# First MLP: one activation function in place of a chain of three, and seven block products in place of eight

## The chip, the cores and the metric

One core of a Trainium2 chip runs the whole program. The metric is the device time of that core in microseconds (us), lower is better; before the change the median of 3 runs is 575.84 us (575.25 to 576.12). TensorE (PE) multiplies, VectorE (DVE), ScalarE (ACT) and GpSimd (POOL) work element by element, SyncE (SP) issues the transfers. Products land in PSUM, everything else lies in SBUF.

## The reference

A decaying linear attention over 2 x 768 tokens gives x (1536 x 512), and two MLPs follow:

```
h = x @ w_in                       # 512 -> 2048
sp = where(h > 20, h, log1p(exp(min(h, 20))))
x = (h * tanh(sp)) @ w_out         # 2048 -> 512
h = x @ w_in2
r = maximum(h, 0)
out = (r * r) @ w_out2
```

The function h * tanh(softplus(h)) of the first MLP is known as Mish. All arrays are fp32, and the result has to be as exact as fp32 allows.

## The kernel before

Each fp32 operand is split into a high part (rounded, type fp32r) and a low part (what is left): ACT copies the high part, DVE subtracts (`split`, L248). A product of two such operands is three matmuls: high by low, low by high, high by high (`mm3`). All matmuls of the MLPs are 128 x 128 (stationary) by 128 x 512 (moving).

The 1536 tokens are three blocks t = 0, 1, 2 of 512. The hidden 2048 channels are four groups g of 512. For each MLP (L = 0, 1) and each group the kernel loads and splits two weight tiles for the way up (kind 0) and two for the way down (kind 1), forms h (`up`), applies the activation and splits the result (`take`, `gated`), multiplies down (`down`) and adds to an accumulator (`ac`). `up` of one block is 48 matmuls, and so is `down` of one block.

The second MLP already takes blocks 1 and 2 together (`up_pair`): with the block matrices of the weights and of x it forms seven products P1, P2, P6, P7, P5, P4, P3 (a Strassen-Winograd scheme) of 12 matmuls each, 84 in place of 96. For that DVE forms four differences T1 to T4 of the x blocks once per MLP (`forms`; seven operands are then split into fh and fl), four sums S of the weights once per group (`sums`; tiles s, then sh and sl), and seven additions per group that put the products together (tiles u and h). `STRASSEN` (L33) says which MLP does so.

The first MLP's activation before is a chain: DVE takes min(h, 20) into z (L568), ACT applies Sigmoid, Arctan and Sin to z (L571), DVE multiplies h by z, then the split gives gh and gl. Sigmoid and Arctan share one table set of ACT, Sin has another, so ACT loads tables (ACT_TABLE_LOAD).

The order of the work is set by a planner (`Plan`) when the program is built: each operation has an assumed duration, TensorE's have a rank, the others a due time derived from it; the planner gives each engine a fixed list, and 50 SBUF units of 128 x 1024 and four PSUM pairs of banks to the tiles. On the chip every engine works its list strictly in order and waits on semaphores. `LATE` says how many of a group's three `down` come after the next group's `up` of block 0.

Names: attention works on 12 chunks of 128 tokens; sc are its scores, a the masked scores, sd the state update, xo its output in PSUM, kv and qk the inputs; xh, xl are the split x, xr the x kept whole (block pair), st, m and t are weights as loaded and being decoded (L490, L493, L498), wh and wl the split weights, dn the product down, yh and yl the split input of the second MLP.

Of the kernel before, what the change touches and what calls it, by code (L numbers as in the profile page):

```python
# [12 lines left out]
F32 = mybir.dt.float32  # L13
# [4 lines left out]
ALU = mybir.AluOpType  # L18
# [11 lines left out]
RANGE = 2.0 ** -112  # L30

UNITS = 50
STRASSEN = (False, True)  # L33
DEBUG = None
SPARE = (10, 6)
AHEAD = 40.0
LATE = (1, 1, 0, 0)


class Val:  # L40
# [5 lines left out]


class Op:
    def __init__(self, eng, us, fn, name, rank, table, lag, due, spare):
        self.eng, self.us, self.fn, self.name, self.rank, self.table = eng, us, fn, name, rank, table  # L50
        self.lag, self.due, self.spare = lag, due, spare
        self.before, self.after, self.vals = {}, {}, {}
        self.late, self.start, self.end = math.inf, None, None


class Plan:
# [11 lines left out]
        self.ops, self.ahead = [], ahead  # L68
        self.wrote, self.used, self.orders = {}, defaultdict(list), set()

    def op(self, eng, us, fn, reads=(), writes=(), name="", rank=None, table=None, lag=None, due=None, spare=0):
        o = Op(eng, us, fn, name, rank, table, self.LAG[eng] if lag is None else lag, due, spare)
        for x in reads:
            o.before[self.wrote[x]] = None
        for x in writes:
            o.before.update(dict.fromkeys(self.used[x]))
            if x in self.wrote:
                o.before[self.wrote[x]] = None
        for x in reads:
            self.used[x].append(o)  # L80
        for x in writes:
            self.wrote[x], self.used[x] = o, []
        for x in (*reads, *writes):
            if isinstance(x[0], Val):
                o.vals[x[0]] = None
        for v in o.vals:
            v.left += 1
        for b in o.before:
            b.after[o] = None
        self.ops.append(o)  # L90
        return o
# [29 lines left out]
    def run(self, start, units):  # L121
        self.dues(start)
        free = {"S": list(range(units)), "P": list(range(4))}
        clock = dict.fromkeys(self.LAG, 0.0)
        left = {o: len(o.before) for o in self.ops}
        ready = {e: [] for e in self.LAG}
        for o in self.ops:
            if not left[o]:
                o.at = 0.0
                ready[o.eng].append(o)  # L130
        releases, table, order = [], [None], []
        now, n = 0.0, 0
        while n < len(self.ops):
            while releases and releases[0][0] <= now:
                _, v = releases.pop(0)
                free[v.space].append(v.slot)
            for e in ready:
                if clock[e] > now:
                    continue
                can = [o for o in ready[e] if o.at <= now and (e == "PE" or o.late - now < self.ahead[e])]  # L140
                if not can:
                    continue
                best = None
                for o in sorted(can, key=lambda o: o.rank if e == "PE" else
                                o.late + (2.6 if o.table and table[0] not in (None, o.table) else 0.0)):
                    need = defaultdict(int)
                    for v in o.vals:
                        if v.slot is None:
                            need[v.space] += 1
                    if all(len(free[s]) >= k + (o.spare if s == "S" else 0) for s, k in need.items()):  # L150
                        best = o
                        break
                if best is None:
                    continue
                o = best

                if e != "PE" and any(q.at > now and q.at < now + 0.7 * o.us and q.late < o.late - 2.0
                                     for q in ready[e]):
                    continue
                us = o.us  # L160
                if o.table:
                    us += 1.3 if table[0] != o.table else 0.0
                    table[0] = o.table
                for v in sorted((v for v in o.vals if v.slot is None), key=lambda v: v.name):
                    v.slot = free[v.space].pop(0)
                o.start, o.end = now, now + us
                clock[e] = o.end
                ready[e].remove(o)
                order.append(o)
                n += 1  # L170
                for v in o.vals:
                    v.left -= 1
                    v.was = max(v.was or 0.0, o.end + o.lag)
                    if not v.left:
                        bisect.insort(releases, (v.was, v), key=lambda r: r[0])
                for a in o.after:
                    left[a] -= 1
                    if not left[a]:
                        a.at = max(b.end + (b.lag if (b.eng != a.eng or b.lag > 1) and (b, a) not in self.orders else 0.0)
                                   for b in a.before)  # L180
                        ready[a.eng].append(a)
            times = [c for c in clock.values() if c > now]
            times += [o.at for r in ready.values() for o in r if o.at > now]
            times += [r[0] for r in releases[:1]]
            times += [o.late - self.ahead[e] + 1e-6 for e in ready if e != "PE" for o in ready[e]
                      if o.late - self.ahead[e] + 1e-6 > now]
            times = [t for t in times if t > now]
            if not times:
                stuck = [o.name for r in ready.values() for o in r][:20]
                held = sorted({v.name for o in self.ops for v in o.vals if v.slot is not None and v.left and v.space == "S"})  # L190
                raise RuntimeError(f"stuck {held} at {now} with {n} of {len(self.ops)}: {stuck} {len(free['S'])} {len(free['P'])}")
            now = min(times)
        self.order = order
        return order
# [3 lines left out]
def attention_mlps(ctx, tc, lam, qk, kv, w_in, w_out, w2_in, w2_out, out):  # L198
# [15 lines left out]
    NG = DFF // (GF * P)  # L214
    assert DM == NP * P and DM == TB and NK == GF == 4 and SEQ % 2 == 0 and NB == 3

    const = ctx.enter_context(tc.tile_pool(name="const", bufs=1))
    units = ctx.enter_context(tc.tile_pool(name="units", bufs=1))
    banks = ctx.enter_context(tc.tile_pool(name="banks", bufs=1, space=PSUM))
    dram = ctx.enter_context(tc.tile_pool(name="dram", bufs=1, space=bass.MemoryType.DRAM))  # L220
# [50 lines left out]


    W = 2 * CH
    neg_ln2 = const.tile([P, 1], F32, name="neg_ln2")
    tab_d = dram.tile([H, W], F32, name="tab_d")
    misc = Val("misc")
    mask = Val("mask")
# [34 lines left out]
    def ones():  # L312
        nc.vector.memset(tab()[:, 0 : CH - 1], 0.0)
        nc.vector.memset(tab()[:, CH - 1 : CH], 1.0)
        nc.vector.memset(neg_ln2, -math.log(2.0))

    op("ACT", 0.1, lambda: nc.scalar.dma_start(out=tab()[:, CH : CH + 1], in_=lam), [], [(misc, "lam")],
       name="lam", lag=2.2, due=0.0)
    op("DVE", 0.4, ones, [], [(misc, "tab"), ("neg_ln2", 0)], name="ones")
    op("DVE", 1.2, powers, [(misc, "lam")], [(misc, "tab")], name="powers")  # L320
    op("ACT", 0.1, lambda: nc.scalar.dma_start(out=tab_d, in_=tab()), [(misc, "tab")], [("tab_d", 0)],
       name="tab_d", lag=2.2, due=0.0)
# [236 lines left out]
    def gated(L, g, t, u, h, in_psum):  # L559

        name = f"{L}{g}{t}{u}"
        hi, lo = Val(f"gh{name}", dtype=F32R), Val(f"gl{name}", dtype=F32R)
        g_hi[L, g, t, u], g_lo[L, g, t, u] = hi, lo
        if L == 0:


            z = Val(f"z{name}")
            op("DVE", 0.8, lambda: nc.vector.tensor_scalar(  # L568
                out=tl(z), in0=tl(h), scalar1=20.0, scalar2=None, op0=ALU.min), [(h, 0)], [(z, 0)], name=z.name)
            for f, table, kw in ((AF.Sigmoid, "s", {"bias": neg_ln2}), (AF.Arctan, "s", {}), (AF.Sin, "t", {"scale": 2.0})):  # L570
                op("ACT", 1.05, lambda f=f, kw=kw: nc.scalar.activation(out=tl(z), in_=tl(z), func=f, **kw),  # L571
                   [(z, 0), ("neg_ln2", 0)], [(z, 0)], name=f"{f}{name}", table=table)
            op("DVE", 1.25, lambda: tt(tl(h), tl(h), tl(z), ALU.mult), [(h, 0), (z, 0)], [(h, 0)], name=f"g{name}")
        else:
            if not in_psum:
                op("ACT", 1.05, lambda: nc.scalar.activation(out=tl(h), in_=tl(h), func=AF.Relu),
                   [(h, 0)], [(h, 0)], name=f"r{name}")
            op("ACT", 1.05, lambda: nc.scalar.activation(out=tl(h), in_=tl(h), func=AF.Square),
               [(h, 0)], [(h, 0)], name=f"sq{name}")
        split(hi, lo, h, [(h, 0)])  # L580

    def take(L, g, t, u, src):
        h = Val(f"h{L}{g}{t}{u}")
        op("ACT", 1.05, lambda: nc.scalar.activation(out=tl(h), in_=tl(src), func=AF.Relu if L else AF.Copy),  # L584
           halves(src), [(h, 0)], name=h.name)
        gated(L, g, t, u, h, True)

# [242 lines left out]
```

## Time and profile before

| | |
|---|---|
| median of 3 runs | 575.84 us (575.25 to 576.12) |
| profiled execution | 575.08 us, its span 573.0 us |
| PE busy | 558.7 us (98%), 2970 matmuls |
| DVE busy | 378.8 us (66%) |
| ACT busy | 369.2 us (64%), of it 56.5 us in 44 table loads |
| POOL busy | 33.1 us (6%) |

The span is what the profiler saw from the first to the last instruction; the remaining 2.08 us lie around it. The attention fills the first 71 us, together with the first block's `up`; then the first MLP runs to about 319 us and the second to the end. Busy shares are averages over these stages; ends of matmuls are modelled, since they are pipelined: a matmul shows 389 ns, but the next one starts after 227 ns.

### The profile page before, as it was taken

How to read it: one execution, taken by the hardware profiler on the slowest of the kernel's cores; microseconds unless marked ns; L12 is line 12 of the kernel's file. 1: busy time of each engine (PE TensorE's matmuls, PEld its weight loads, DVE VectorE, ACT ScalarE, POOL GpSimd, SP SyncE). 2: the span in 40 equal slices, each digit the busy share in tenths (PEclk: the TensorE clock that was granted, in tenths of full speed). 3: DMA queues.
4: the chain of work that ended last, by engine and by line, in shares of the span. 5: the costliest groups of instructions: out<-in, count | busy, mean ns of one | idle time of the engine just before them, and what ended most of it. 6: DMA issues, size and time to landing. Idle time of an engine off the chain costs nothing.

```text
span 573.0 us, 7150 instructions
## 1 busy us (share of the span) xinstructions
PE 558.7 (98%) x2970; PEld 462.2 (81%) x2970; DVE 378.8 (66%) x414; ACT 369.2 (64%) x390; POOL 33.1 (6%) x31
## 2 busy tenths in 40 slices
PE   5899999999999999999999999999999999999997
PEld 2778888888888888888888887888888888888885
DVE  5656896358557686476398989852858677497622
ACT  2436678999978987987989678554624556147600
POOL 1564500000000000000000000000000000000000
PEclk9999999999999999999999999999999999999999
DMA  7998040401204031040303002021140123200022
GB/s 233 398 409 338 3 129 19 139 9 45 103 1 148 2 110 38 0 148 0 120 28 122 25 1 73 1 74 38 60 160 1 37 74 114 107 1 1 1 110 110
DMA packets 15999, 50.53 MB, mean 88 GB/s; under 512 B 1624, under 2 KB 3168, under 8 KB 15968
## 3 DMA queue, kind: packets, MB, share of 16 engines
q1 hardware_dynamic: 15936, 50.08, 25.0%
q8 instruction: 23, 0.38, 0.3%
q14 instruction: 8, 0.07, 0.0%
q10 hardware_dynamic: 32, 0.01, 0.0%
HBM read 46.92 MB, written 3.15 MB: 87 GB/s over the span
## 4 chain that ended last, share of the span: by engine, by line
PE 94%; DMA 2%; DVE 2%; SPq 1%; ACT 1%; issue 0%
PE dn L260 46%; PE up L260 31%; PE p L260 12%; PE sc L375 2%; PE xo L416 2%; PE xo L420 2%; DMA qk<-in_qk_dram 1%; PE sd L398 1%; DMA tab_d<-misc 1%; DVE t L498 0%; DVE misc L306 0%; SPq L334 0%; DMA misc<-in_lam_dram 0%; DVE u L253 0%; DVE wl L253 0%
## 5 line engine op out<-in xcount | busy, mean ns | idle before, releaser
L253 DVE TENSOR_TENSOR ac<-dn,ac 128x1024 f32<-128x1024 f32 (+1 forms) x38 | 44.4, 1168 | 68.2 <-PE dn L260 68.2
L498 DVE SCALAR_TENSOR_TENSOR t<-m,t 128x1024 int32<-128x1024 int32 x64 | 77.0, 1221 | 4.7 <-ACT m L490 3.8
L260 PE MATMUL up<-xh,wh 128*128 128x512 f32 x192 | 75.1, 391 | 0.7 <-ACT xh L250 0.7
L260 PE MATMUL up<-xl,wh 128*128 128x512 f32 x192 | 75.1, 391 | 0.5 <-DVE xl L253 0.5
L260 PE MATMUL dn<-wl,gh 128*128 128x512 f32 x192 | 74.8, 389 | 0.2 <-DVE wl L253 0.2
L260 PE MATMUL up<-xh,wl 128*128 128x512 f32 x192 | 74.7, 389 | 0.0
L260 PE MATMUL dn<-wh,gl 128*128 128x512 f32 x192 | 74.7, 389 | 0.0
L260 PE MATMUL dn<-wh,gh 128*128 128x512 f32 x192 | 74.7, 389 | 0.0
L260 PE MATMUL dn<-gl,wh 128*128 128x512 f32 x192 | 74.7, 389 | 0.0
L260 PE MATMUL dn<-gh,wl 128*128 128x512 f32 x192 | 74.7, 389 | 0.0
L260 PE MATMUL dn<-gh,wh 128*128 128x512 f32 x192 | 74.7, 389 | 0.0
L253 DVE TENSOR_TENSOR gl<-h,gh 128x1024 fp32r<-128x1024 f32 x48 | 58.3, 1221 | 17.7 <-ACT gh L250 17.7
L584 ACT ACTIVATE h<-up 128x1024 f32<-128x1024 f32 x32 | 32.9, 1027 | 41.7 <-PE up L260 41.7
L250 ACT ACTIVATE wh<-t 128x1024 fp32r<-128x1024 f32 x32 | 33.3, 1052 | 39.9 <-DVE t L498 39.9
L571 ACT ACT_TABLE_LOAD x44 | 56.5, 1283 | 0.8
L250 ACT ACTIVATE gh<-h 128x1024 fp32r<-128x1024 f32 x48 | 50.4, 1055 | 6.6 <-DVE h L253 5.9
L571 ACT ACTIVATE z<-z 128x1024 f32<-128x1024 f32 x48 | 50.8, 1060 | 0.8
L490 ACT ACTIVATE m<-st 128x512 f32<-128x512 f32 x64 | 39.4, 658 | 6.1 <-DMA st<-in_moe_w_in_dram 5.0
L260 PEld LDWEIGHTS up<-xl,wh 128*128 128x128 f32 x192 | 36.0, 188 | 8.7 <-DVE xl L253 0.9
L260 PEld LDWEIGHTS up<-xh,wh 128*128 128x128 f32 x192 | 36.0, 188 | 8.5 <-ACT xh L250 0.9
L260 PEld LDWEIGHTS dn<-wl,gh 128*128 128x128 f32 x192 | 36.0, 188 | 8.1 <-PE p L260 0.6
L253 DVE TENSOR_TENSOR wl<-t,wh 128x1024 fp32r<-128x1024 f32 x32 | 38.7, 1219 | 5.4 <-ACT wh L250 5.3
(78 smaller groups left out, 947.1 us busy)
## 6 DMA issues: line engine op xcount, KB each, us to landing
st<-in_moe_w_in_dram SPq DMA_DIRECT2D x32, 512.0 KB, 4.5
st<-in_moe_w_out_dram SPq DMA_DIRECT2D x32, 512.0 KB, 3.9
qk<-in_qk_dram SPq DMA_DIRECT2D x12, 512.0 KB, 10.4
kv<-in_kv_dram SPq DMA_DIRECT2D x12, 512.0 KB, 10.2
out_dram<-ac SPq DMA_DIRECT2D x4, 512.0 KB, 2.8
out_dram<-ac SPq DMA_DIRECT2D x4, 256.0 KB, 2.0
mask<-tab_d SPq DMA_DIRECT2D x2, 256.0 KB, 3.9
misc<-tab_d SPq DMA_DIRECT2D x2, 128.0 KB, 6.3
```

The lines of the kernel that those rows point to most:

```text
L250: nc.scalar.activation(out=o, in_=i, func=AF.Copy)
L253: nc.vector.tensor_tensor(out=o, in0=a, in1=b, op=alu)
L260: nc.tensor.matmul(out=out_, lhsT=a, rhs=b, start=first and i == 0, stop=last and i == 2)
L375: nc.tensor.matmul(out=o[:, e, p], lhsT=t[r, 1, p], rhs=t[r, 0, p], start=True, stop=True)
L398: nc.tensor.matmul(out=o[e * D : (e + 1) * D, p], lhsT=t[:, p, 1 + e], rhs=t[:, p, 0 if e else 3], start=True, stop=True)
L416: nc.tensor.matmul(out=o[e * D : (e + 1) * D, p, n], lhsT=v[:, p, 0 if e else 3], rhs=w[:, e, p], start=True, stop=fresh)
L420: nc.tensor.matmul(out=o[r, p, n], lhsT=z[:, p, r], rhs=qd[:, p], start=False, stop=True)
L490: op("ACT", 0.67, lambda st=st, i=i: nc.scalar.activation(out=tl(m)[:, i], in_=tl(st, TB, 2)[:, :, 1].bitcast(F32), func=AF.Copy, scale=RA ...
L498: nc.vector.scalar_tensor_tensor(out=tl(t), in0=tl(m).bitcast(I32), scalar=scalar, in1=tl(t), op0=shift, op1=ALU.bitwise_or)
L571: op("ACT", 1.05, lambda f=f, kw=kw: nc.scalar.activation(out=tl(z), in_=tl(z), func=f, **kw), [(z, 0), ("neg_ln2", 0)], [(z, 0)], name=f" ...
L584: op("ACT", 1.05, lambda: nc.scalar.activation(out=tl(h), in_=tl(src), func=AF.Relu if L else AF.Copy), halves(src), [(h, 0)], name=h.name)
```

## The change

The first MLP's activation becomes one ACT function, Mish, straight from PSUM to SBUF (`take`) or in place (`gated`); the chain of z, the constant and the planner's account of tables go. `STRASSEN` is set for the first MLP also, so blocks 1 and 2 go through `forms`, `sums` and `up_pair` there, and the x of these blocks is kept whole (xr) in place of being split as it comes. `LATE` becomes zero for all, so a group's three `down` follow its products directly, in both MLPs.

```diff
-STRASSEN = (False, True)
+STRASSEN = (True, True)
-LATE = (1, 1, 0, 0)
+LATE = (0, 0, 0, 0)
...
-        if L == 0:
...
-            z = Val(f"z{name}")
-            op("DVE", 0.8, lambda: nc.vector.tensor_scalar(
-                out=tl(z), in0=tl(h), scalar1=20.0, scalar2=None, op0=ALU.min), [(h, 0)], [(z, 0)], name=z.name)
-            for f, table, kw in ((AF.Sigmoid, "s", {"bias": neg_ln2}), (AF.Arctan, "s", {}), (AF.Sin, "t", {"scale": 2.0})):
-                op("ACT", 1.05, lambda f=f, kw=kw: nc.scalar.activation(out=tl(z), in_=tl(z), func=f, **kw),
-                   [(z, 0), ("neg_ln2", 0)], [(z, 0)], name=f"{f}{name}", table=table)
-            op("DVE", 1.25, lambda: tt(tl(h), tl(h), tl(z), ALU.mult), [(h, 0), (z, 0)], [(h, 0)], name=f"g{name}")
-        else:
-            if not in_psum:
-                op("ACT", 1.05, lambda: nc.scalar.activation(out=tl(h), in_=tl(h), func=AF.Relu),
-                   [(h, 0)], [(h, 0)], name=f"r{name}")
+        if not in_psum:
+            op("ACT", 1.05, lambda: nc.scalar.activation(out=tl(h), in_=tl(h), func=AF.Relu if L else AF.Mish),
+               [(h, 0)], [(h, 0)], name=f"r{name}")
+        if L:
             op("ACT", 1.05, lambda: nc.scalar.activation(out=tl(h), in_=tl(h), func=AF.Square),
                [(h, 0)], [(h, 0)], name=f"sq{name}")
...
     def take(L, g, t, u, src):
-        op("ACT", 1.05, lambda: nc.scalar.activation(out=tl(h), in_=tl(src), func=AF.Relu if L else AF.Copy),
+        op("ACT", 1.05, lambda: nc.scalar.activation(out=tl(h), in_=tl(src), func=AF.Relu if L else AF.Mish),
```

How the lists move is shown at three places. The names carry the program's numbers: MLP, group, then kind or block; fl06 is the low part of the operand of P6 in MLP 0, p600 its product, and a10, a11 are the last two of the attention's 12 chunks.

First TensorE around the attention's last chunk (xo5 with a11). Before:

```order
L260 MATMUL up0010_741<-xl10_516,wh0000_132 128x512
...
L416 MATMUL xo5_711<-a11_709,kv11_445 64x128 x2
...
L260 MATMUL up0011_804<-xl10_516,wh0000_132 128x512
...
L260 MATMUL up0020_844<-xl20_734,wh0000_132 128x512
...
L260 MATMUL dn00000_865<-gl0000_857,wh0010_840 128x512
```

Now:

```order
L254 MATMUL p100_739<-fl01_689,wh0000_127 128x512
...
L408 MATMUL xo5_719<-a11_717,kv11_452 64x128 x2
...
L254 MATMUL p200_779<-fl02_746,wh0001_354 128x512
...
L254 MATMUL p600_818<-fl06_810,sh000_407 128x512
...
L254 MATMUL dn00000_925<-gl0000_917,wh0010_767 128x512
L254 MATMUL dn00000_925<-gh0000_588,wl0010_921 128x512
```

Behind the last chunk stood block 1's `up` (36 matmuls more, on operands of earlier chunks), and stands now the rest of P1 and P2 (18 matmuls on earlier chunks), and then P6, which needs the last chunk.

Then DVE in the same place. Before:

```order
L253 TENSOR_TENSOR a11_709<-sc11_687,mask_117 128x1024
L253 TENSOR_TENSOR xl20_734<-xo4_631,xh20_707 128x2x256
L253 TENSOR_TENSOR xl21_736<-xo4_631,xh21_728 128x2x256
L253 TENSOR_TENSOR state1_128<-sd5_698,state1_128 64x4x64 x2
L498 SCALAR_TENSOR_TENSOR t0010_501<-m0010_528,t0010_501 128x1024 x2
L253 TENSOR_TENSOR h0000_420<-h0000_420,z0000_464 128x1024
```

Now:

```order
L247 TENSOR_TENSOR a11_717<-sc11_692,mask_112 128x1024
L247 TENSOR_TENSOR state1_123<-sd5_705,state1_123 64x4x64 x2
L247 TENSOR_TENSOR fl02_746<-xr11_518,fh02_637 128x1024
L490 SCALAR_TENSOR_TENSOR t0010_507<-m0010_524,t0010_507 128x1024
L485 TENSOR_SCALAR t0011_765<-st00110_494 128x512
L485 TENSOR_SCALAR t0011_765<-st00111_520 128x512
L490 SCALAR_TENSOR_TENSOR t0011_765<-m0011_566,t0011_765 128x1024
L247 TENSOR_TENSOR T01_786<-xr20_703,xr10_505 128x1024
L247 TENSOR_TENSOR T02_796<-xr21_714,T01_786 128x1024
L247 TENSOR_TENSOR T03_802<-xr21_714,xr20_703 128x1024
L247 TENSOR_TENSOR fl06_810<-T02_796,fh06_804 128x1024
```

The differences T and their low parts stand now between the last chunk and P6.

Last DVE ahead of the first `down` (dn00000). Before:

```order
L253 TENSOR_TENSOR h0001_541<-h0001_541,z0001_662 128x1024
L253 TENSOR_TENSOR wl0010_840<-t0010_501,wh0010_799 128x1024
L253 TENSOR_TENSOR gl0000_857<-h0000_420,gh0000_802 128x1024
L253 TENSOR_TENSOR wl0011_861<-t0011_795,wh0011_838 128x1024
L253 TENSOR_TENSOR gl0001_863<-h0001_541,gh0001_842 128x1024
```

Now:

```order
L247 TENSOR_TENSOR fl03_889<-xr21_714,fh03_814 128x1024
L247 TENSOR_TENSOR h0021_897<-p500_862,u200_880 128x1024
L247 TENSOR_TENSOR u100_858<-p500_862,u100_858 128x1024
L490 SCALAR_TENSOR_TENSOR t0011_765<-m0011_566,t0011_765 128x1024
L247 TENSOR_TENSOR gl0000_917<-h0000_425,gh0000_588 128x1024
L247 TENSOR_TENSOR wl0010_921<-t0010_507,wh0010_767 128x1024
L247 TENSOR_TENSOR h0011_923<-p400_882,u200_880 128x1024
L247 TENSOR_TENSOR gl0001_938<-h0001_545,gh0001_649 128x1024
L247 TENSOR_TENSOR wl0011_941<-t0011_765,wh0011_919 128x1024
```

What the first `down` reads (gl0000, wl0010) stands now behind all that the seven products need.

## Rows read from the trace of the kernel before

**Rows 1.** Chain that ended last, in order of time: start us, us, what.

```profile
32.60 8.00 PE up L260 x34
...
62.62 1.09 PE sc L375 x16
...
66.07 2.94 PE up L260 x12
69.02 0.37 PE xo L416 x4
...
70.91 11.10 PE up L260 x48
82.02 10.88 PE dn L260 x48
...
392.52 19.04 PE p L260 x84
...
569.36 0.69 DVE ac L253
```

**Rows 2.** Waits of PE over the span: for whom, us, times, longest us.

```profile
PE xo L416 <- DMA kv<-in_kv_dram: 4.9, 1, 4.9
...
PE dn L260 <- DVE wl L253: 0.2, 1, 0.2
```

**Rows 3.** Groups by shape: name, shapes, count | busy us, mean ns | idle before.

```profile
L571 ACT ACTIVATE z<-z 128x1024 f32<-128x1024 f32 x48 | 50.8, 1060 | 0.8
...
L260 PEld LDWEIGHTS up<-xh,wl 128*128 128x128 f32 x192 | 36.0, 188 | 7.2
...
L253 DVE TENSOR_TENSOR s<-s,t 128x512 f32<-128x512 f32 x4 | 2.8, 694 | 0.1
```

**Rows 4.** Busy by stretch: us, PE, PEld, DVE, ACT, POOL, granted clock, DMA.

```profile
9.00:12.00 3.00, 0.00 (x0) 0.00 (x0) 1.87 (x2) 1.06 (x1) 0.00 (x0) 1.00 0.92 266
12.00:15.00 3.00, 1.53 (x15) 1.56 (x16) 2.36 (x2) 0.00 (x0) 1.50 (x1) 1.00 1.07 357
...
329.54:569.40 239.86, 239.60 (x1056) 197.77 (x1055) 158.50 (x161) 115.61 (x122) 0.00 (x0) 1.00 0.17 56
```

**Rows 5.** DVE in order of time: start us, us, operation, count.

```profile
13.23 1.22 DVE L253 TENSOR_TENSOR wl<-t,wh 128x1024 fp32r<-128x1024 f32 x1
...
63.76 1.22 DVE L253 TENSOR_TENSOR a<-sc,mask 128x1024 f32<-128x1024 f32 x1 [0.34 <-PE sc L375]
64.90 1.28 DVE L253 TENSOR_TENSOR xl<-xo,xh 128x512 fp32r<-128x512 f32 x2
66.09 0.86 DVE L253 TENSOR_TENSOR state<-sd,state 64x256 f32<-64x256 f32 x2
66.99 2.48 DVE L498 SCALAR_TENSOR_TENSOR t<-m,t 128x1024 int32<-128x1024 int32 x2
...
70.53 0.42 DVE L493 TENSOR_SCALAR t<-st 128x512 int32<-128x512 int32 x1
...
310.75 2.35 DVE L253 TENSOR_TENSOR wl<-t,wh 128x1024 fp32r<-128x1024 f32 x2
```

**Rows 6.** ACT in order of time, as the attention ends.

```profile
70.96 1.09 ACT L250 ACTIVATE xh<-xo 128x512 fp32r<-128x512 f32 x2 [2.71 <-PE xo L420]
71.93 1.06 ACT L250 ACTIVATE wh<-t 128x1024 fp32r<-128x1024 f32 x1
72.88 1.06 ACT L250 ACTIVATE gh<-h 128x1024 fp32r<-128x1024 f32 x1
```

**Rows 7.** POOL in order of time, two equal operations.

```profile
13.50 1.86 POOL L381 TENSOR_TENSOR kv<-kv,mask 128x512 f32<-128x512 f32 x1 [10.93 <-DMA kv<-in_kv_dram]
...
19.94 1.06 POOL L381 TENSOR_TENSOR kv<-kv,mask 128x512 f32<-128x512 f32 x1 [0.28 <-DMA kv<-in_kv_dram]
```

**Rows 8.** PE in order of time, equal work early and late.

```profile
13.47 1.98 PE L416 MATMUL xo<-a,kv 128*64 128x128 f32 x16 [4.89 <-DMA kv<-in_kv_dram]
...
52.02 1.05 PE L416 MATMUL xo<-a,kv 128*64 128x128 f32 x16
```

More of the change, by code (lines that the diff above doesn't have):

```diff
@@ L48, with __init__ @@
 class Op:
-    def __init__(self, eng, us, fn, name, rank, table, lag, due, spare):
-        self.eng, self.us, self.fn, self.name, self.rank, self.table = eng, us, fn, name, rank, table
+    def __init__(self, eng, us, fn, name, rank, lag, due, spare):
+        self.eng, self.us, self.fn, self.name, self.rank = eng, us, fn, name, rank
         self.lag, self.due, self.spare = lag, due, spare
@@ L69, in __init__, with op @@
         self.wrote, self.used, self.orders = {}, defaultdict(list), set()
-    def op(self, eng, us, fn, reads=(), writes=(), name="", rank=None, table=None, lag=None, due=None, spare=0):
-        o = Op(eng, us, fn, name, rank, table, self.LAG[eng] if lag is None else lag, due, spare)
+    def op(self, eng, us, fn, reads=(), writes=(), name="", rank=None, lag=None, due=None, spare=0):
+        o = Op(eng, us, fn, name, rank, self.LAG[eng] if lag is None else lag, due, spare)
         for x in reads:
@@ L130, in run @@
                 ready[o.eng].append(o)
-        releases, table, order = [], [None], []
+        releases, order = [], []
         now, n = 0.0, 0
@@ L143, in run @@
                 best = None
-                for o in sorted(can, key=lambda o: o.rank if e == "PE" else
-                                o.late + (2.6 if o.table and table[0] not in (None, o.table) else 0.0)):
+                for o in sorted(can, key=lambda o: o.rank if e == "PE" else o.late):
                     need = defaultdict(int)
@@ L159, in run @@
                     continue
[L160 to L163, printed above, removed]
                 for v in sorted((v for v in o.vals if v.slot is None), key=lambda v: v.name):
                     v.slot = free[v.space].pop(0)
-                o.start, o.end = now, now + us
+                o.start, o.end = now, now + o.us
                 clock[e] = o.end
@@ L215, in attention_mlps @@
     assert DM == NP * P and DM == TB and NK == GF == 4 and SEQ % 2 == 0 and NB == 3
-    const = ctx.enter_context(tc.tile_pool(name="const", bufs=1))
     units = ctx.enter_context(tc.tile_pool(name="units", bufs=1))
@@ L273, in attention_mlps @@
     W = 2 * CH
-    neg_ln2 = const.tile([P, 1], F32, name="neg_ln2")
     tab_d = dram.tile([H, W], F32, name="tab_d")
@@ L314, in ones @@
         nc.vector.memset(tab()[:, CH - 1 : CH], 1.0)
-        nc.vector.memset(neg_ln2, -math.log(2.0))
     op("ACT", 0.1, lambda: nc.scalar.dma_start(out=tab()[:, CH : CH + 1], in_=lam), [], [(misc, "lam")],
        name="lam", lag=2.2, due=0.0)
-    op("DVE", 0.4, ones, [], [(misc, "tab"), ("neg_ln2", 0)], name="ones")
+    op("DVE", 0.4, ones, [], [(misc, "tab")], name="ones")
     op("DVE", 1.2, powers, [(misc, "lam")], [(misc, "tab")], name="powers")
```

## The prediction

> **What bounds the kernel now.** I read four views in this order: busy shares and stretches, the waits of PE, the chain that ended last, and then DVE, ACT and POOL in order of time where the attention ends.
>
> The chain [rows 1] is what to look at first. From 32.60 us to the last addition at 569.36 it is TensorE's matmuls, almost without a break, and 48 of them (one `up` or `down` of a block) take 10.88 us wherever they stand, 84 take 19.04: 0.2267 us each. TensorE's waits behind 32.6 us come to almost nothing [rows 2]: the long one, 4.9 us, is for an early transfer, and the one that stands alone in the MLPs is 0.2 us. So what is taken off TensorE's list comes off the time, as long as no new wait takes its place; what is taken off ACT is worth nothing by itself.
>
> **The change part by part.**
>
> *Products.* Four groups of the first MLP need 84 matmuls in place of 96 for blocks 1 and 2: 4 x 12 x 0.2267 = 10.88 us less [rows 1]. The seven-product form has the same pace already in the second MLP (84 in 19.04).
>
> The Trainium skill (Perfetto Trace Analysis, Identifying the Most-Contended Engine) says that matmul occupancy is no good measure and weight-load occupancy a better one. By it one would count 48 weight loads of 188 ns [rows 3], 9.0 us, for the removed work. The row speaks against it here: the next matmul starts after 227 ns everywhere, so 10.88 us; the difference is 1.9 us.
>
> *Activation.* 72 ACT functions, 44 table loads and 48 DVE operations on z and h go; 24 Mish and one more table load come. ACT was hidden behind TensorE before, so this is worth 0 us. Mish stands in no row: I bound one between a copy's 1.05 us [rows 6] and three functions' 3 x 1.06 = 3.2 us [rows 3], and take 1.06, the nearest rows, since Sigmoid, Arctan and Sin share one mean. At 3.2 the only place without cover is the first group, where Mish of P2's sum stands ahead of fh04 on ACT; that has some 2 us to spare, so 0 to 2 us more. A gain is excluded, ACT being off the path.
>
> *The same scheme in groups 1 to 3.* DVE gets per group four sums S of 0.69 [rows 3], two sl and seven additions of 1.22, and loses six operations on z and six multiplications: about even, in 276 x 0.2267 = 62.6 us of products. What is queued behind these additions was tried out by the second MLP: over 239.86 us with seven products in every group TensorE was busy 239.60 us [rows 4]. I take 0 us, bounded by that 0.26 for each group.
>
> *LATE.* Block 2's `down` now follows block 1's directly. Its operand comes from the last product by addition, function, copy, subtraction, 1.22 + 1.06 + 1.05 + 1.22 = 4.6 us; in front stand two `down`, 21.8 us, as cover. 0 us in both MLPs. If that cover were one `down`, 10.9 us would still do.
>
> *The filling of the first group.* This is the only part that costs. P6, P7, P5 and P4 need T1 to T4, and so the attention's last chunk; DVE gets 11 operations of about 1.22 us (four T, seven fl) for eight xl of 0.64 [rows 5], and they fall into a few microseconds. I follow the new lists with the durations of before.
>
> TensorE: at 66.07 [rows 1] the first half of P1 stands in place of 12 `up` matmuls that took 2.94 (12 x 0.2267 = 2.72, so 0.22 for the turn): 1.36 + 0.22 gives 67.65. The last chunk's xo takes 70.91 - 69.02 = 1.89: 69.54. The rest of P1 and P2, 18 matmuls and a turn, 4.30: 73.84. From here TensorE wants P6.
>
> DVE: mask of chunk 11, whose scores end at 62.62 + 1.09 [rows 1], from 63.76 to 64.95, state 0.86, fl02 1.13 (two such follow each other in 2.35 less the overlap [rows 5]), bits 1.2, t twice 0.42, bits 1.2: free at 70.15. The xl pair and h by z that stood there are gone.
>
> ACT: two copies out of xo begin 0.05 us after its end [rows 6], so 69.59, first done at 70.2, second at 70.68. T1 starts at 70.25, T2 at 71.4, ready at 72.6. ACT copies P1 out (71.15 to 72.1), then fh05, then fh06 at 73.05 (0.95 from one to the next [rows 6]), ready at 74.1. fl06 runs 74.15 to 75.4. P6 starts at 75.4: **a wait of 1.6 us**.
>
> From fl06 on DVE is the busy one. Twelve operations stand between fl06 and wl0010 (fl07, h of P2, T4, fl05, u, fl04, u, fl03, h of P5, u, bits, gl0000), so wl0010 starts at 74.15 + 13 x 1.13 + 0.07 = 88.9 and is ready at 90.1. The five products from 75.4 need 60 x 0.2267 = 13.6 us, until 89.0; each of their operands is ready before its turn (fl05 at 79.9 for 80.8, fl04 at 82.2 for 83.6, fl03 at 84.4 for 86.3). The first `down` needs wl0010: **a wait of 1.1 us**. Its second half needs wl0011, three operations later, 93.5, and is due at 95.5.
>
> Bounds of the first wait: 0, if DVE and ACT run 1.6 us ahead of my count, and 10.6, if TensorE had to wait until all seven operands are split (fl03 at 84.4). Of the second: 0, and 3.4, if wl0011 were needed first. I take the counted values, since every duration has a row.
>
> POOL feeds the same place (state and q of the last chunks). An equal operation took 1.06 us alone and 1.86 beside a DVE operation with two SBUF inputs, wl at 13.23 [rows 5, 7]. The change puts S, fl01 and fl02, of that kind, into the attention. The Trainium skill (SBUF — State Buffer, SBUF: two separate sides) says that the two engines hold a shared port by an exclusive lock for a whole instruction; the trace agrees, 0.80 us of delay. By it the last xo could come 0.8 us late for each collision; by the list it has 67.65 - 65.8 = 1.85 us to spare, so 0 us by either, but less room.
>
> **Sum.** -10.88 + 1.6 + 1.1 = -8.2 us. Against the profiled execution (span 573.0 us and 2.08 around it, 575.08) that is 566.9. It stands 0.76 below the median of the runs, 575.84, so I predict 567.6.
>
> **Rivals.**
>
> *The filling is hidden.* DVE and ACT get ahead by the idle time they have before the last chunk; both waits vanish: 575.84 - 10.9 = 565.0. For it: ACT is far emptier now, DVE had idle pieces. Against: T2 hangs on the last xo by a chain without slack, which no head start shortens.
>
> *The filling costs double.* TensorE's pace falls after a wait. For it: the sixteen xo matmuls behind the idle 4.89 us took 1.98 us, equal ones at 52.02 only 1.05 [rows 8], so about half pace. The granted clock reads 1.00 (the 2.4 GHz level) there too [rows 4]. The Trainium skill (TensorE: Matmul & The Clock Gate, Part 1) says that the clock is halved after idleness; the granted clock of no row shows that, the pace does. Against: my waits are a third of that. Price: some 2 us for each wait (0.93 for sixteen of the small ones, and the same again for what follows), 567.6 + 4 = 571.6. Late masks through POOL would give a similar sum.
>
> *The change does not do what it says.* A wait elsewhere gives all of the 10.88 back, or Mish is slow in every group: 575.8. Against: in the second MLP, with the same scheme and one function more for each tile, ACT is busy 115.61 of 239.86 us [rows 4].
>
> *Slower.* P6 waits for all seven operands, not its own two, because DVE and ACT stand in another order of need or lag by 9 us: then 10.6 + 1.1 are lost against 10.88, 576.7. It decides from a first wait of 9.8 us on. For it: strict lists, and by my count twenty DVE operations in a row without a pause. Against: P6 stands behind fl06 alone in the list, with fl03 seven operations later.
>
> **How the numbers follow.** Forecast 66%: waits of 1 to 5 us, 565.9 to 569.9. Hidden 10%. Double 17%. No effect 3%. Slower 4%. The range 564.6 to 571.6 leaves out the upper part of the third case and the last two. A difference under 0.2% (1.15 us) is about what a measurement of this kernel cannot tell from no change; faster by more holds for the first three cases, 93%.
>
> **What would show it.** In the chain: `p` x84 in 19.04 us in eight places in place of four. In TensorE's waits: one for fl of the first group's P6 (1.6 us, at about 74 us), one of `dn` for wl (1.1 us, at about 89 us), none over 0.3 us behind 100 us. ACT: two table loads, Mish near 1.06 us. Wrong would be the forecast with a wait in the later groups, with a Mish above 3 us, or with matmuls at half pace behind the waits.

## The result and the profile after

The changed kernel takes 568.05 us (median of 4 runs, 566.86 to 568.88) against 575.79 us before: the ratio is 0.9865, 95% interval 0.9844 to 0.9886, so 7.7 us less. 567.6 was predicted.

The chain that ended last, in order of time (start us, us, what), of the profiled execution (568.5 us, span 566.7), answers to [rows 1]:

```profile
33.15 8.01 PE up L254 x34
...
66.85 1.58 PE p L254 x6
68.43 0.37 PE xo L408 x4
...
70.33 1.60 PE p L254 x6
71.95 0.67 ACT u L244
72.62 0.25 issue
72.88 1.05 ACT fh L244
74.01 1.07 ACT fh L244
75.10 1.24 DVE fl L247
76.47 10.03 PE p L254 x36
86.52 1.23 DVE h L247
...
91.14 1.15 DVE wl L247
92.33 32.75 PE dn L254 x143
125.08 10.88 PE up L254 x48
135.96 19.04 PE p L254 x84
155.00 32.64 PE dn L254 x144
...
563.04 0.69 DVE ac L247
```

Behind 92.33 there is nothing but matmuls at their old pace, 84 products in 19.04 us for each later group of both MLPs. The change keeps its gain there. Nearly all of the loss lies between 70 and 92 us: TensorE waits for fh and fl of P6's operand, then P6, P7 and P5 (36 matmuls) take 10.03 us where 8.16 would do, and then DVE brings h, ... wl before the first `down` (92.33 is its second matmul, the one that reads wl; the first ran at 91.76). Another 0.55 us stands ahead of the first `up` in the chain, 33.15 for 32.60, and is not of the change: in the profiles of the variants below that place lies anywhere from 32.48 to 35.22. The waits of TensorE (us, times, longest) name the same, beside [rows 2]:

```profile
PE p L254 <- DVE fl L247: 1.8, 1, 1.8
...
PE dn L254 <- DVE wl L247: 0.2, 1, 0.2
```

The first wait is there; the second is only 0.2 us. Why it is so short shows in the stretches (us, PE, PEld, DVE, ACT, POOL, granted clock, DMA), beside [rows 4]:

```profile
73.00:76.00 3.00, 1.63 (x8) 1.01 (x6) 2.95 (x3) 2.90 (x3) 0.00 (x0) 1.00 0.00 0
76.00:79.00 3.00, 2.53 (x8) 2.02 (x9) 2.97 (x4) 2.49 (x5) 0.00 (x0) 0.70 0.00 0
79.00:82.00 3.00, 3.00 (x11) 2.42 (x10) 2.85 (x3) 2.93 (x4) 0.00 (x0) 0.73 0.00 0
82.00:85.00 3.00, 3.00 (x15) 2.48 (x14) 2.69 (x4) 1.02 (x2) 0.00 (x0) 1.00 0.00 0
```

Right behind the wait the granted clock is 0.70 and 0.73 on average, a mixture of the two levels 1.2 and 2.4 GHz: from 77.26 to 80.25 us one matmul starts 0.43 us after the other, and from 80.65 on 0.23 us again. TensorE reached the first `down` so late that DVE was almost ready.

ACT (line, operation, out<-in, count | busy us, mean ns | idle before) has 260.1 us to do in place of 369.2:

```profile
L557 ACT ACTIVATE h<-h 128x1024 f32<-128x1024 f32 x32 | 33.9, 1059 | 58.8 <-DVE h L247 58.8
L566 ACT ACTIVATE h<-up 128x1024 f32<-128x1024 f32 x16 | 16.5, 1029 | 36.3 <-PE up L254 36.3
L482 ACT ACT_TABLE_LOAD x1 | 1.3, 1283 | 4.2 <-DVE misc L299 4.2
L566 ACT ACT_TABLE_LOAD x1 | 1.3, 1283 | 0.0
```

The first two groups hold Mish of the first MLP and Relu of the second. Taken by time, the 13 in place between 95 and 320 us, all Mish, have a median of 1.06 us, the 16 Relu behind 320 us the same. So Mish costs what the others cost, with two table loads in all.

### The profile page after: what moved, and what is told of

It is laid out like the page before. It is cut to its first block, busy times and chain, and to the rows that moved or that the text cites. A ratio compares the mean times of both kernels' runs of the same rounds, so it can differ in the third digit from the quotient of the medians.

```text
span 566.7 us, 7023 instructions
## 1 busy us (share of the span) xinstructions
PE 549.7 (97%) x2922; PEld 454.1 (80%) x2922; DVE 398.9 (70%) x420; ACT 260.1 (46%) x294; POOL 34.9 (6%) x31
## 4 chain that ended last, share of the span: by engine, by line
PE 94%; DMA 2%; DVE 2%; ACT 1%; SPq 1%; issue 0%; ACTq 0%
PE dn L254 46%; PE p L254 26%; PE up L254 15%; PE sc L367 2%; PE xo L408 2%; PE xo L412 2%; DMA qk<-in_qk_dram 1%; PE sd L390 1%; DMA tab_d<-misc 1%; ACT fh L244 0%; DVE misc L299 0%; DMA misc<-in_lam_dram 0%; SPq L326 0%; DVE fl L247 0%; DVE h L247 0%
## 5 line engine op out<-in xcount | busy, mean ns | idle before, releaser
L247 DVE TENSOR_TENSOR h<-p,u 128x1024 f32<-128x1024 f32 x32 | 39.2, 1224 | 33.5 <-PE p L254 33.5
L557 ACT ACTIVATE h<-h 128x1024 f32<-128x1024 f32 x32 | 33.9, 1059 | 58.8 <-DVE h L247 58.8
L254 PE MATMUL p<-fl,sh 128*128 128x512 f32 x128 | 50.6, 395 | 1.8 <-DVE fl L247 1.8
L254 PE MATMUL p<-fh,sl 128*128 128x512 f32 x128 | 50.5, 394 | 0.0
L254 PE MATMUL p<-fh,sh 128*128 128x512 f32 x128 | 50.3, 393 | 0.0
L254 PEld LDWEIGHTS dn<-gh,wl 128*128 128x128 f32 x192 | 36.0, 188 | 8.1 <-DVE wl L247 0.6
L254 PEld LDWEIGHTS dn<-wh,gl 128*128 128x128 f32 x192 | 36.0, 188 | 7.5
L254 PEld LDWEIGHTS dn<-gh,wh 128*128 128x128 f32 x192 | 36.0, 188 | 7.5
## 6 DMA issues: line engine op xcount, KB each, us to landing
kv<-in_kv_dram SPq DMA_DIRECT2D x12, 512.0 KB, 10.2
```

The lines of the kernel that those rows point to most:

```text
L247: nc.vector.tensor_tensor(out=o, in0=a, in1=b, op=alu)
L254: nc.tensor.matmul(out=out_, lhsT=a, rhs=b, start=first and i == 0, stop=last and i == 2)
```

## Experiments

**Mish alone.** Eight products and the old LATE, but Mish in place of the chain.

```diff
-STRASSEN = (True, True)
+STRASSEN = (False, True)
-LATE = (0, 0, 0, 0)
+LATE = (1, 1, 0, 0)
```

> Mish alone, eight products in the first MLP as before. Theory A (TensorE's list is the bound, ACT's relief is worth nothing): 575.8 us, within 0.5, though ACT's busy time falls by some 90 us. Rival B (part of the gain comes from ACT and its 44 table loads): 569 to 573.

Measured: 575.33 us, ratio to before 1.0005 (0.9995 to 1.0015); ACT busy 240.3 us. Theory A holds: 129 us less on ACT (some 90 were expected) are worth nothing by themselves.

**Seven products alone.** The kernel before with two constants changed; the chain Sigmoid, Arctan, Sin stays.

```diff
-STRASSEN = (False, True)
+STRASSEN = (True, True)
-LATE = (1, 1, 0, 0)
+LATE = (0, 0, 0, 0)
```

> Seven products and LATE zero alone, with the old chain of three functions. Theory A: the products bring their 10.88 us less the filling; DVE has the z and h operations on top in the filling, so its waits grow from 2.7 to 4 to 7 us: 569 to 572. Rival B: without Mish the gain is lost, 574 or more, since ACT with its table loads holds up the second half of each group.

Measured: 592.92 us, ratio 1.0308 (1.0294 to 1.0322). Theory A's number is wrong by over 20 us; rival B has the sign, though I had not thought of the size. TensorE's waits (us, times, longest):

```profile
PE dn L260 <- DVE gl L253: 14.3, 4, 5.2
...
PE dn L260 <- DVE wl L253: 4.5, 1, 4.5
```

The waits lie in several groups, and most of the loss is in the first: from its first `up` to the next group's it takes 104.1 us, against 87.8 in the version without waits further below. Its chain (start us, us, what):

```profile
94.58 10.82 PE dn L260 x36
105.43 1.03 ACT ac L250
106.47 1.28 ACT L571
107.76 2.00 ACT z L571 x2
...
111.65 1.24 DVE gl L253
112.93 23.69 PE dn L260 x96
```

Ahead of 94.58 DVE has no pause (busy 21.73 of the 22 us from 72 to 94), and TensorE waits 5.2 us for gl. The second wait, 4.8 us, ends at 112.93 behind a chain over ACT, which copies a finished `down` (ac), loads a table and then applies the functions. Behind both waits TensorE is slow as well: the 36 matmuls take 10.82 us in place of 8.16, at a granted clock of 0.77. The second group has no wait, the third and the fourth one of 2.2 us each, and the wait for wl is in the second MLP's first group. The third group, its chain, then DVE and TensorE (with the idle time ahead and what ended it):

```profile
229.09 19.14 PE dn L260 x84
248.26 1.23 DVE ac L253
249.49 2.27 DVE h L253 x2
251.75 1.22 DVE gl L253
253.11 12.75 PE dn L260 x48
```

```profile
248.26 1.23 DVE L253 TENSOR_TENSOR ac<-dn,ac 128x1024 f32<-128x1024 f32 x1 [1.35 <-PE dn L260]
249.41 2.35 DVE L253 TENSOR_TENSOR h<-h,z 128x1024 f32<-128x1024 f32 x2
251.74 2.42 DVE L253 TENSOR_TENSOR gl<-h,gh 128x1024 fp32r<-128x1024 f32 x2
253.11 0.64 PE L260 MATMUL dn<-gl,wh 128*128 128x512 f32 x1 [2.17 <-DVE gl L253]
```

DVE's list has an accumulator's addition, which waits for a `down`, ahead of h by z, which the next `down` waits for. DVE had been idle 1.35 us ahead of that addition; TensorE has 12 matmuls left when it starts, and then stands for 2.2 us. The 48 `down` matmuls behind it take 12.75 us in place of 10.88.

**The same without table loads.** Sin becomes Arctan, so that all three stand in one set; against the run above the lists differ by the loads alone, 2 in place of 33, so 31 fewer. It computes another function.

```diff
...
-(AF.Sin, "t", {"scale": 2.0})
+(AF.Arctan, "t", {"scale": 2.0})
...
```

> Seven products with the old chain of three functions, but the third is Arctan again in place of Sin, so that all stand in one table set; the lists are the same but for 33 table loads less (another function is computed). Theory T (the table loads of 1.28 us make the chain late for the downs): most of the 17.6 us over the kernel before goes, 575 to 580. Rival Z (DVE's two operations more for each tile and the length of the chain do it): 587 or more.

Measured: 593.73 us, ratio 1.0303 (1.0272 to 1.0333). Theory T falls: without the loads the time is no shorter. The load in the first group's chain is gone, and the waits for gl sum to 13.0 us in place of 14.3, but the matmuls behind the first group's waits take 1.1 us more (11.03 and 24.57 for 10.82 and 23.69). Rival Z's number is met, which does not show its reason.

**The same chain with the old LATE.** Seven products in both MLPs, LATE (1, 1, 0, 0), the rest as before the change.

> Seven products with the old chain, and LATE as before, so that in groups 0 to 2 block 2's down has the next group's up in front of it, 10.88 us more for the chain of z. Theory Q (without Mish the chain, 10 us long and queued behind the accumulators' additions, comes too late for downs that follow directly; not the loads, not the amount of work): the waits of about 5 us in the later groups go, 575 to 583. Rival W (DVE and ACT have too much work in any order): 588 or more.

Measured: 611.36 us, ratio 1.0611 (1.0584 to 1.0637). Theory Q falls: more cover made it worse (waits of `dn` for gl 25.7 us in 5 places). Rival W's number is met; its reason is not shown. Over longer stretches both engines have time left (between 135 and 200 us DVE is busy 45.4 and ACT 43.0 of 65 us), but in places DVE has none: 13.67 of the 14 us from 226 to 240, where the chain runs through it. The same rows as above stand in the chain, ac, h twice, gl, at 178.96 and at 250.90. So the loads are not the reason. A DVE that is full where a group's products are put together, and the place of ac in the lists, are both read from the traces; neither was tried apart, and what each costs stays open.

**LATE as before in the changed kernel.**

```diff
-LATE = (0, 0, 0, 0)
+LATE = (1, 1, 0, 0)
```

> The changed kernel with LATE as before (block 2's down behind the next group's up). Theory A: no wait hung on it, 568.0 us, within 0.6. Rival C (the order of the downs is part of the gain): 1 us or more above 568.

Measured: 566.64 us (566.53 to 567.01), ratio 0.9849 (0.9836 to 0.9863). That is 1.4 us under the first median of the changed kernel, beyond what A allowed, and not what C said. No wait stands behind the filling. The filling itself differs: TensorE waits 1.7 us for fl, nearly as long, but runs at full clock behind it (the stretches as above):

```profile
73.00:76.00 3.00, 1.33 (x6) 0.83 (x5) 3.00 (x4) 2.91 (x4) 0.00 (x0) 1.00 0.00 0
76.00:79.00 3.00, 3.00 (x14) 2.44 (x14) 2.97 (x3) 1.96 (x3) 0.00 (x0) 1.00 0.00 0
```

The first `down` starts at 90.57, 58.0 us behind the chain's first `up` (32.56), against 59.2 us in the changed kernel (33.15 to 92.33). It starts behind a wait of 0.6 us for wl.

**The changed kernel again.** No edit, on the chip and beside the runs of the two experiments that follow.

> The changed kernel itself once more, with a second profile. Theory K (after the wait for P6 the matmuls run at half pace in some executions and at full pace in others): the times spread again over 566.5 to 569, and the profile shows either P6, P7, P5 in 10.0 us with the first down at about 92 us, or in 8.2 us with a wait of 1.1 us and the first down at about 91. Rival P (half pace always, so the variant with LATE as before owes its 1.4 us to its order): each profile shows 10.0 us, and the times stay near 568.

Measured: 567.35 us (566.83 to 568.33), ratio 0.9848 (0.9823 to 0.9874). The profiled execution is the one of 568.33 us, again with 10.05 us for P6, P7, P5, a granted clock of 0.64 and 0.79 behind the wait, and the first `down` at 92.19. With the first four runs, nine times of the changed kernel lie in two lots: 566.83 to 567.60 (six) and 568.33 to 568.88 (three). Both profiles are from the upper lot. Theory K fits, as the slow pace is worth 1.2 us, and the mean granted clock of a whole execution parts the lots in the same way: 0.987 in each of the upper three, 0.99 to 1.00 in the lower six. That the lower six ran P6, P7 and P5 at full pace stands in no profile. The median of 568.05 lies between the lots; no execution took that time.

**Matmuls with no use in the gap.** Eight more matmuls ahead of P6, whose sums are overwritten.

```diff
+            if fill:
+                def again():
+                    for _ in range(fill):
+                        nc.tensor.matmul(out=tl(o)[:, 0], lhsT=tl(w_hi[L, g, 0, 1])[:, 0, 0:P],
+                                         rhs=tl(f_hi[L, 2])[:, 0], start=True, stop=True)
...
```

> Eight matmuls with no use (their sums are overwritten) stand between P2 and P6 of the first group, 1.8 us. Theory K: TensorE is not idle there, the half pace never comes; P6 still starts when fl06 is there, the wait ahead of the first down is about 1 us, 566.5 to 567.2 with little spread. Rival P (the pace falls for another reason than the wait): 568 and 10.0 us for P6, P7, P5 as before.

Measured: 567.16 us (566.87 to 568.78), ratio 0.9852 (0.9827 to 0.9876); no difference from the changed kernel in time. In the trace the slow pace is gone:

```profile
77.16 13.89 PE p L254 x60
91.05 32.69 PE dn L254 x144
```

Five products take 13.89 us (13.6 at the old pace) and the granted clock is 1.00 in all of these stretches. P6 starts 0.9 us later than in the changed kernel's second profile (77.16 for 76.30), since the planner, with one more operation, put DVE's h ahead of fl06; the first `down` follows 58.2 us behind the first `up`. The idea holds for this profile; since the pace falls only in some executions, one profile does not prove it. One of the five executions, 568.78 us, has the mean granted clock of the upper lot, 0.987, where the profiled one has 0.990; so it is not shown that the eight matmuls keep the clock up every time.

**State scaling on ACT.** POOL gives up the state's scaling.

```diff
-                if t:
+                if False:
...
-                op("POOL" if t else "ACT", 1.3 if t else 1.2, scale, ...
+                op("ACT", 1.2, scale, ...
```

> The attention's state scaling goes from POOL to ACT in all chunks. Theory S (POOL and DVE hold each other up; s, fl01 and fl02 took 1.4 to 1.7 us in place of 0.7 and 1.2): some of these DVE operations fall back to 0.7 and 1.2, P6 starts 0.3 to 0.6 us earlier against the last chunk, 567.0 to 568. Rival (the chain over the last chunk sets P6, not DVE's queue): P6 keeps its distance, time within 0.3 of the changed kernel's.

Measured: 568.63 us (567.45 to 570.44), ratio 0.9876 (0.9845 to 0.9907): no gain. DVE (start us, us, operation) of the changed kernel first, then of this one:

```profile
61.34 1.67 DVE L247 TENSOR_TENSOR fl<-xr,fh 128x1024 fp32r<-128x1024 f32 x1
...
66.99 1.38 DVE L247 TENSOR_TENSOR fl<-xr,fh 128x1024 fp32r<-128x1024 f32 x1
```

```profile
59.21 1.23 DVE L247 TENSOR_TENSOR fl<-xr,fh 128x1024 fp32r<-128x1024 f32 x1
...
65.78 1.23 DVE L247 TENSOR_TENSOR fl<-xr,fh 128x1024 fp32r<-128x1024 f32 x1
```

Theory S is right about the collisions (1.67 and 1.38 became 1.23) and wrong about the time: P6 starts 75.26 - 69.30 = 5.96 us behind the last xo in place of 6.14, and what was won there returns as waits for gl and wl at the first `down` (1.1 us ahead of 90.25 and 0.6 us ahead of 91.29). DVE's queue, not P6, sets that `down`. The planner also moved one `t` of 1.2 us in DVE's list from ahead of T1 (70.22 us in the changed kernel) to ahead of gl (86.49, two in a row), so the price of the collisions is not parted from this move.

**Block 0's down between P2 and P6.** In the first group alone.

```diff
-                       name=f"P{i}{L}{g}{s}", rank=rank + count[0])
+                       name=f"P{i}{L}{g}{s}", rank=rank + 5 * count[0])
...
-                up_pair(L, g, ranks())
+                r = ranks()
+                up_pair(L, g, r)
+                if (L, g) == (0, 0):
+                    down(*downs.pop(0), r + 16)
...
```

> In the first group block 0's down stands between P2 and P6, 10.88 us of products that need nothing of the last chunk. Theory A (only the two waits of the filling and what follows from them keep the change from its full 10.88): both waits go, the half pace behind them too, 564.9 to 565.6, no wait of TensorE over 0.3 us behind 40 us. Rival D (DVE is the bound of the filling, whatever stands in the list): the wait moves to another place and the time stays at 567 to 568.

Measured: 564.44 us (563.74 to 564.96), ratio 0.981 (0.9797 to 0.9823): 10.88 us less than before (575.32 in the same comparison; by the interval of the ratio 10.2 to 11.7), which is the whole of the products' price. The chain:

```profile
32.93 8.00 PE up L254 x34
...
70.09 4.30 PE p L254 x18
74.40 10.88 PE dn L254 x48
85.28 13.60 PE p L254 x60
98.88 21.88 PE dn L254 x96
120.76 10.88 PE up L254 x48
```

No wait, no slow matmul. Theory A holds, with a time 0.5 us under its range; rival D falls. This version beats both kernels.

## Why the prediction was right

*Products.* -10.88 us, and the variant with block 0's `down` moved got 10.88. The term was right; that it agrees to the last digit is luck, with an interval of 10.2 to 11.7. The weight loads' 9.0 us lie outside that interval.

*Activation.* 0 us for Mish held against the kernel before (575.33 for 575.32), and Mish took the 1.06 us that were assumed. (The row of 1.06 us that three functions were priced from holds 48 operations, so two of the three; the one with the constant takes 1.15. Nothing hung on it.) But it was priced as if each part stood alone. The seven products by themselves cost 17.6 us (592.92), with Mish they gain 7.7. Mish is what lets the products' gain through. The step that said "ACT was hidden behind TensorE before, so this is worth 0 us" is true of eight products only; nothing in the forecast depended on it, and yet it would have misled whoever took the change apart.

*Groups 1 to 3 and LATE.* 0 us each; TensorE stands nowhere behind the first `down`. The cover of 21.8 us was ample for Mish's 4.6. The old LATE is no worse, and with the long chain neither LATE fits.

*The filling.* 1.6 + 1.1 = 2.7 us was forecast. The first wait was 1.8. The second was 0.2, as the matmuls behind the first one lost 10.03 - 8.16 = 1.87 us to a lower clock. To compare the sum, take the distance from the first `up` to the first `down`: 98.88 - 10.88 - 32.93 = 55.1 us in the version without waits, 59.2 in the two profiles of the changed kernel, 58.0 with the old LATE, which ran the same filling at full clock. The end of the group's last `down` says the same: 125.08 - 33.15 = 91.9 us behind the first `up` in the changed kernel, 120.76 - 32.93 = 87.8 without waits. So the filling costs 2.9 us at full clock, as counted, and 4.1 with the slow stretch. The mis-sized term is the second wait: 1.1 us of waiting for DVE became 0.2 us of waiting and 1.9 us of slow matmuls. The prediction had named matmuls at half pace behind the waits as a sign against itself, and in the profiled executions that sign came. That the time stayed near the forecast even there is partly luck: the slow stretch ran while DVE was still at work for the first `down`, and so took the place of most of a wait that was counted already.

*Rivals.* "The filling costs double" was half right: its mechanism came after a wait a little over a third as long as the one it was read from, against my doubt (the row behind it was no clean sign, see the last section), but behind one wait only and for 1.2 us, not for 4, since part of the slow stretch lay beside a wait for DVE that was due anyway. "The filling is hidden" needed another order, as the last experiment shows: the head start of DVE and ACT did nothing for T2, which hangs on the last xo. "The change does not do what it says" did not occur, but it is what the seven products do without Mish. The slower case did not occur either: P6 waited for fl06 alone. The POOL collisions came as the rows said, on DVE's side also, and were paid out of DVE's queue.

## What to carry to other kernels

When one engine bounds a kernel, count its instructions for the gain, and look for the cost where the new scheme starts: there the operands of many products hang on one late input. Work that needs nothing of that input, set between, was worth more here than making the late chain faster. And test the parts of a change together: a relief worth nothing alone can be what another part needs.

## What the runs showed of the hardware

- TensorE's clock can fall behind waits of about 2 us, and does not always. In two profiles of the changed kernel the granted clock fell behind waits of 1.84 and 1.83 us (0.70 and 0.73, 0.64 and 0.79 in the stretches behind them); behind 1.67 and 1.62 us in two variants it stayed at 1.00. The length of the wait does not decide by itself: the seven products alone have two waits of 2.17 us, and the granted clock is 0.87 behind the first (253.1 to 266.0 us) and 1.00 behind the second (319.7 to 331.0).
- The row that I had read the loss of pace from, sixteen xo behind a wait of 4.9 us [rows 8], was no clean sign: in the kernel before, the sixteen `sc` ahead of that wait are slow already, 2.08 us for 1.16 at 18.73 us. In the changed kernel fourteen `sc` ahead of the same place take 0.95 us, and the sixteen xo behind it 1.98 again, now with a granted clock of 0.50 from 10 to 15 us. The kernel before shows the same 1.98 us beside a granted clock of 1.00 [rows 4], so there the pace tells more than the record of the clock. The kernel before, TensorE with the idle time ahead:

```profile
6.50 2.08 PE L375 MATMUL sc<-qk 64*128 64x128 f32 x16 [0.87 <-DMA qk<-in_qk_dram]
```

- DVE's operations with two SBUF inputs get longer themselves beside POOL: fl 1.67 us for 1.23, and in the changed kernel two of the weight sums 1.44 and 1.55 us for 0.69. I had priced only POOL's side [rows 7].
- 31 table loads of 1.28 us fewer did not shorten a kernel that ACT's chain held up in its first group (593.73 against 592.92 us).
